# The first block of x is loaded from SyncE's queue, third, and no longer from ScalarE's

## The chip, the cores and the metric

The kernel runs on one core of a Trainium2 chip. The core has five engines that run their own instruction streams: TensorE (PE in the profile; its weight loads are PEld), VectorE (DVE), ScalarE (ACT), GpSimd (POOL) and SyncE (SP). Transfers are issued by an engine into its queue and carried by 16 DMA engines. The metric is the device time of one execution in microseconds (us).

## The reference

A depthwise convolution with a 1x1 window, and then a pointwise one. The depthwise weight is a scale for each channel, so that it can be put into the matrix of the pointwise one.

```python
x: (1, 384, 384, 384) bf16     # 147,456 pixels of 384 channels
dw: (1, 1, 384), pw: (384, 384)
out = xp[:, i:i+H, j:j+W, :] * dw[i, j]          # one tap, k = 1
return jnp.einsum('bhwc,cd->bhwd', out, pw)
```

## The kernel before

The 147,456 pixels are cut into 288 *supertiles* of 512 pixels (384 KB of x, and as much output). A *chunk* is a run of supertiles loaded by one transfer: 1, 1, 2, 2, 4 supertiles, then 26 chunks of 10, then 6, 4, 4, 2, 1, 1. The first chunk is called x0 here, the next x1, and so on. There are three large buffers for x (`Xs`) and three for the output (`Os`), used in turn by groups of 10 supertiles; the last two supertiles have a buffer of their own (`Xl`), loaded by ScalarE.

The weights are prepared on the chip. pw comes by two loads on SyncE: its first 128 rows (L150, 96 KB, semaphore `s_pw`) and the other 256 (L151, 192 KB, `s_pw2`). dw comes by a load on ScalarE (L149). TensorE turns dw into a column (L225), VectorE builds three scaled selection matrices from it (`sel_w`, L310), and TensorE multiplies them with the rows of pw (L245): step k = 0 needs the first load of pw, k = 1 and 2 the second. The products are six pieces in PSUM; ScalarE casts pieces 0, 2, 3, 4, 5 into `w_r` and VectorE piece 1 (L295). Ahead of that TensorE runs matmuls on constants (`idle_work`, L212) that nothing reads.

Each supertile then goes through three engines. VectorE transposes it in two halves (L282, `transposes`), which wait for its chunk's semaphore and for TensorE to be done with the buffer `T` two supertiles before. TensorE does 12 steps of 4 matmuls that work side by side on 32 rows each (L195, `supertile`); the first step waits for the first half of the transpose, for a free PSUM buffer and, in the very first supertile, for pieces 0 to 3 of the weights; pieces 4 and 5 are waited for in later steps. ScalarE copies the PSUM buffer to the output buffer (L332).

SyncE issues all other loads and the stores in one written order: `todo` is sorted by the supertile after which each may go. Loads x1 to x4 go at once; before the first chunk of 10 SyncE waits for x1 to land (L162); then that chunk and the next go, and then 28 waits on a semaphore that is long full (L166), which let SyncE pass without a pause; then stores and loads alternate. A load into a buffer in use waits for the last transpose that reads it (L121), a store for ScalarE's copy (L145). Each engine's transfers go into one queue of its own: SyncE's is q1, ScalarE's q10.

The step that the change touches is the issue of x0 (L152), a call of `load_x` with ScalarE as the issuing engine; without that argument `load_x` issues from SyncE. x0 is waited for by the first transposes.

Of the kernel before, what the change touches and what calls it, by code (L numbers as in the profile page):

```python
# [27 lines left out]
def kernel(  # L28
# [12 lines left out]
    nc = tc.nc  # L41
# [61 lines left out]
    with tc.tile_critical(sync_engine=mybir.EngineType.Pool, no_gpsimd_drain=True):  # L103
        def x_of(t):
            g, i, off, first, L = chunks[t]
            n = first + LONG - NS
            if n >= 0:
                return Xl[:, 4 * n : 4 * n + 4, :], s_xl[n], 16
            n = sum(len(ls) > i for ls in groups[g % NR : g + 1 : NR])
            return Xs[g % NR][:, 4 * off : 4 * (off + L), :], s_x[g % NR][i], 16 * n  # L110

        def load_x(t, eng=nc.sync):
            g, i, off, first, L = chunks[t]
            dst, sem, _ = x_of(t)
            rows = xf[512 * first : 512 * (first + L), :]
            if first + LONG < NS:
                src = rows.rearrange("(p s) c -> p (s c)", p=P)
                dst = dst.rearrange("p s c -> p (s c)")
                if i == 0 and g >= NR:
                    je = g_end[g - NR]  # L120
                    eng.wait_ge(s_t[je % 2][1], je // 2 + 1)  # L121
            else:
                src = rows.rearrange("(a k q) c -> q a k c", k=4, q=4)
            eng.dma_start(dst, src).then_inc(sem, 16)
# [24 lines left out]
        nc.scalar.dma_start(dw_row[:], dw.rearrange("a e c -> a (e c)")).then_inc(s_dw, 16)  # L149
        nc.sync.dma_start(pw_n[:, 0], pw[0:P, :]).then_inc(s_pw, 16)  # L150
        nc.sync.dma_start(pw_n[:, 1:3], pw[P:C, :].rearrange("(k p) d -> p k d", p=P)).then_inc(s_pw2, 16)  # L151
        load_x(0, nc.scalar)  # L152

        todo = []
        for t, (g, i, off, first, L) in enumerate(chunks):
# [214 lines left out]
```

## Time and profile before

| what | us |
|---|---|
| median of 3 runs | 576.95 (576.24 to 577.43) |
| the profiled execution | 577.43 |
| its span, first to last instruction | 575.7 |
| first matmul of L195 | 8.44 |
| last output copies begin | 571.57 |
| TensorE busy | 567.2 (99%) |
| VectorE busy | 507.0 (88%) |
| ScalarE busy | 419.1 (73%) |
| DMA engines, packet time of q1 | 97.2% of 16 engines' span |

A line of the profile's groups gives the line, the engine and the operation, what is written from what, the shape, the count; then busy time and the mean duration in ns; then the idle time of the engine ahead of it and what ended it. A line of the timeline gives the start, the duration and the same names, with the idle time in brackets. In a table by stretches the columns are the stretch, its length, the engine's busy time and its instructions, the clock granted to TensorE (1.00 is full), the busy share of the DMA engines and GB/s. A line of transfers gives the issuing engine (ACTq is ScalarE's sequencer, SPq SyncE's), the count, the KB of each, and the median time from the issue to the landing. A line on a queue gives its packets, its MB and the time that its packets took as a share of the 16 engines' time.

### The profile page before, as it was taken

To read this page: it belongs to the slowest core of one execution; us is meant where nothing else is said; L and a number is where in the kernel's file an instruction comes from. 1 tells how busy PE (TensorE), PEld (TensorE's weight loads), DVE (VectorE), ACT (ScalarE), POOL (GpSimd) and SP (SyncE) were. 2 spreads that over 40 slices of the span, in tenths; PEclk is the share of its full clock that TensorE was granted. 3 is DMA by queue.
4 is the path that set the end of the run, shared out by engine and by line. 5 is a ranking of instruction groups with operands and counts; after the bars stand their busy time and mean duration, and the time that the engine had idled before them with its cause. 6 is when DMAs were issued, how large, how long until landed. Compare 5 with 4: busy or idle time off the path is not lost.

```text
span 575.7 us, 29705 instructions
## 1 busy us (share of the span) xinstructions
PE 567.2 (99%) x13867; PEld 386.3 (67%) x13867; DVE 507.0 (88%) x584; ACT 419.1 (73%) x297; POOL 0.5 (0%) x5
## 2 busy tenths in 40 slices
PE   7999999999999999999999999999999999999997
PEld 3666666666666666666666666666666666666664
DVE  5889888988898888988898889888988898888985
ACT  5777777777777777777777777777777777777775
POOL 0000000000000000000000000000000000000000
PEclk8999999999999999999999999999999999999999
DMA  8999999999999999999999999999999999999677
GB/s 338 420 366 420 425 422 430 440 416 407 394 425 402 385 396 423 396 388 404 431 381 397 404 424 400 388 419 406 395 404 430 388 403 401 419 394 379 265 287 249
DMA packets 26468, 226.88 MB, mean 394 GB/s; under 512 B 1241, under 2 KB 7002, under 8 KB 22618
## 3 DMA queue, kind: packets, MB, share of 16 engines
q1 hardware_dynamic: 25280, 225.61, 97.2%
q10 hardware_dynamic: 1178, 1.18, 0.7%
q14 instruction: 9, 0.07, 0.0%
q8 instruction: 1, 0.02, 0.0%
HBM read 113.54 MB, written 113.25 MB: 394 GB/s over the span
## 4 chain that ended last, share of the span: by engine, by line
PE 97%; DMA 1%; ACT 1%; issue 0%; DVE 0%; DVEq 0%; SPq 0%; POOLq 0%
PE ps L195 97%; DMA pw_n<-in_pw_dram 1%; DMA out_dram<-O 0%; ACT w_r L295 0%; ACT O L332 0%; DVE O L330 0%; DVEq L103 0%; SPq L150 0%; PE ps L245 0%; SPq L365 0%; POOLq L103 0%; POOLq L354 0%
## 5 line engine op out<-in xcount | busy, mean ns | idle before, releaser
L195 PE MATMUL ps<-w_r,T 32*128 32x384 bf16 x13824 | 563.1, 321 | 0.9 <-ACT w_r L295 0.9
L282 DVE STREAM_TRANSPOSE T<-X 128x384 uint32<-128x384 uint32 x572 | 500.2, 875 | 59.3 <-PE ps L195 1.6
L332 ACT CAST O<-ps 128x1536 bf16<-128x1536 f32 x287 | 413.0, 1439 | 148.4 <-PE ps L195 148.4
L195 PEld LDWEIGHTS ps<-w_r,T 32*128 32x128 bf16 x13824 | 384.9, 93 | 179.1 <-issue 1.2
L295 ACT CAST w_r<-ps 128x768 bf16<-128x768 f32 x5 | 3.7, 810 | 2.5 <-PE ps L245 2.5
L245 PE MATMUL ps<-pw_n,sel_w 64*128 64x384 bf16 x16 | 2.0, 369 | 2.3 <-DMA pw_n<-in_pw_dram 2.2
L282 DVE STREAM_TRANSPOSE T<-Xl 128x384 uint32<-128x384 uint32 x4 | 3.5, 876 | 0.4
L330 DVE CAST O<-ps 128x384 bf16<-128x384 f32 x2 | 1.0, 553 | 3.0 <-DMA out_dram<-O 3.0
L245 PEld LDWEIGHTS ps<-pw_n,sel_w 64*128 64x128 bf16 x16 | 0.7, 97 | 3.9 <-DMA pw_n<-in_pw_dram 3.7
L212 PE MATMUL ps<-const-bfloat16-1.0 32*128 32x384 bf16 x24 | 2.2, 516 | 1.1 <-PEq L354 1.1
L270 ACT ACT_TABLE_LOAD x1 | 1.3, 1283 | 1.9 <-POOLq L103 1.9
L212 PEld LDWEIGHTS ps<-const-bfloat16-1.0 32*128 32x128 bf16 x24 | 0.7, 118 | 1.4 <-issue 1.4
L300 DVE TENSOR_REDUCE sel<-eye 128x64 f32<-128x128 bf16 x1 | 0.3, 286 | 1.5 <-POOL eye L260 1.5
L295 DVE CAST w_r<-ps 128x768 bf16<-128x768 f32 x1 | 1.0, 959 | 0.5 <-PE ps L245 0.5
L329 ACT CAST O<-ps 128x384 bf16<-128x384 f32 x2 | 0.9, 482 | 0.5 <-PE ps L195 0.5
L307 DVE COPY dw_f<-ps 128x3 f32<-128x3 f32 x1 | 0.2, 163 | 0.9 <-PE ps L225 0.9
L310 DVE TENSOR_SCALAR sel_w<-sel,dw_f 128x256 bf16<-128x256 f32 x3 | 0.9, 351 | 0.0
L225 PEld LDWEIGHTS ps<-const-bfloat16-1.0,dw_row 1*128 1x128 bf16 x3 | 0.3, 115 | 0.4 <-DMA dw_row<-in_dw_dram 0.4
L260 POOL TENSOR_SCALAR_AFFINE_SELECT eye<-const-bfloat16-1.0 128x128 bf16<-128x128 bf16 x1 | 0.3, 293 | 0.6 <-POOLq L103 0.6
L270 ACT COPY warm<-const-float32-0.0 128x1 f32<-128x1 f32 x2 | 0.3, 188 | 0.0
L225 PE MATMUL ps<-const-bfloat16-1.0,dw_row 1*128 1x1 bf16 x3 | 0.3, 176 | 0.0
L354 POOL MEMSET const-bfloat16-1.0<- 128x1 bf16 x1 | 0.1, 101 | 0.0
(3 smaller groups left out, 0.3 us busy)
## 6 DMA issues: line engine op xcount, KB each, us to landing
X<-in_x_dram SPq DMA_DIRECT2D x26, 3840.0 KB, 21.4
out_dram<-O SPq DMA_DIRECT2D x26, 3840.0 KB, 27.4
X<-in_x_dram SPq DMA_DIRECT2D x3, 1536.0 KB, 17.9
out_dram<-O SPq DMA_DIRECT2D x4, 768.0 KB, 9.2
out_dram<-O SPq DMA_DIRECT2D x2, 1536.0 KB, 14.9
X<-in_x_dram SPq DMA_DIRECT2D x3, 768.0 KB, 8.3
X<-in_x_dram SPq DMA_DIRECT2D x1, 2304.0 KB, 19.6
out_dram<-O SPq DMA_DIRECT2D x1, 2304.0 KB, 11.4
```

Of the source, the lines that this page charges most:

```text
L195: mm = nc.tensor.matmul(PS[s][:, q, :D], lhsT=Ts[s][32 * q : 32 * q + 32, b, par::2], rhs=w_r[32 * q : 32 * q + 32, b, par, :], start=(b, ...
L212: nc.tensor.matmul(PS[0][:, 2 * (i % 2) + i // 2, :D], lhsT=ones[32 * i : 32 * i + 32, 0:P], rhs=ones[32 * i : 32 * i + 32, :], start=True ...
L225: mm = nc.tensor.matmul(PS[1][:, 0, D + k : D + k + 1], lhsT=dw_row[:, P * k : P * k + P], rhs=ones[0:1, 0:1], start=True, stop=True,)
L245: mm = nc.tensor.matmul(PS[(k + 1) % 2][:, 2 * r + v, :D], lhsT=sel_w[64 * v : 64 * v + 64, k, r, :, :].rearrange("p q w -> p (q w)"), rhs ...
L260: nc.gpsimd.affine_select(out=eye[:], in_=ones[:, 0:P], pattern=[[-1, P]], compare_op=mybir.AluOpType.is_equal, fill=0.0, base=0, channel_ ...
L270: nc.scalar.copy(warm[:, s : s + 1], nc.const_aps.tensor(0.0, [P, 1], F32)).then_inc(s_a[s])
L282: ins = nc.vector.transpose(out=Tw[:, 3 * h : 3 * h + 3], in_=Xw[:, :, j, 96 * h : 96 * h + 96].rearrange("p k (b w) -> p b k w", w=32),)
L295: o = nc.vector.tensor_copy(out, in_) if e == 0 else nc.scalar.copy(out, in_)
L310: nc.vector.tensor_scalar_mul(sel_w[:, k], sel[:].unsqueeze(2).to_broadcast([P, 2, 4, 32]), dw_f[:, k : k + 1]).then_inc(s_sw)
L329: nc.scalar.copy(Ov[:, q, j, :], PS[s][:, q, :D]).then_inc(s_a[s])
L330: nc.vector.tensor_copy(Ov[:, q + 1, j, :], PS[s][:, q + 1, :D]).then_inc(s_d)
L332: a = nc.scalar.copy(Ov[:, :, j, :], PS[s][:, :, :D])
```

## The change

x0 is issued by SyncE, after the two loads of pw and before x1, and no longer by ScalarE after dw. SyncE's queue then holds, in this order, pw's first 128 rows, the other 256, x0, x1, x2, x3, x4. ScalarE's first 28 us hold one transfer, that of dw. Nothing else differs: sizes, buffers, semaphores, the matmuls on constants, the 28 waits on SyncE and the order of the waits at the end are the same.

```diff
         nc.scalar.dma_start(dw_row[:], dw.rearrange("a e c -> a (e c)")).then_inc(s_dw, 16)
         nc.sync.dma_start(pw_n[:, 0], pw[0:P, :]).then_inc(s_pw, 16)
         nc.sync.dma_start(pw_n[:, 1:3], pw[P:C, :].rearrange("(k p) d -> p k d", p=P)).then_inc(s_pw2, 16)
-        load_x(0, nc.scalar)
+        load_x(0)
```

## The prediction

> **What bounds the kernel now.** I read the page first (busy shares and the 40 slices), then the chain that ended last in order of time, then the first 15 us by transfers, by engine and by clock. The page says that TensorE is the bound from end to end:
>
> ```profile
> span 575.7 us, 29705 instructions
> PE 567.2 (99%) x13867; PEld 386.3 (67%) x13867; DVE 507.0 (88%) x584; ACT 419.1 (73%) x297; POOL 0.5 (0%) x5
> PE   7999999999999999999999999999999999999997
> PEclk8999999999999999999999999999999999999999
> L195 PE MATMUL ps<-w_r,T 32*128 32x384 bf16 x13824 | 563.1, 321 | 0.9 <-ACT w_r L295 0.9
> ```
>
> The L195 group has 0.9 us of idle time in the whole run, and all of it lies ahead of its first matmul. So every load after the first few is hidden, and a change to the first loads can act only through the moment at which L195 starts and through the clock just after. Only the first slice has a lower clock (the 8 in PEclk). The chain tells what that start waits for:
>
> ```profile
> 1.40 4.98 DMA pw_n<-in_pw_dram
> 6.42 0.35 PE ps L245 x2
> 6.80 1.51 ACT w_r L295 x2
> 8.44 559.21 PE ps L195 x13063
> ```
>
> The second load of pw is issued at 1.40 and lands at 6.37; two steps of the weight preparation (L245) and two casts (L295) follow, and L195 starts at 8.44. The x0 path ends just before it: in the engine timeline its four transposes begin at 6.57.
>
> ```profile
> 1.52 0.37 ACTq L124 DMA_DIRECT2D X<-in_x_dram  x1
> 1.87 6.31 SPq L124 DMA_DIRECT2D X<-in_x_dram  x6
> 6.41 0.76 PEld L245 LDWEIGHTS ps<-pw_n,sel_w 64*128 64x128 bf16 x12 [2.92 <-DMA pw_n<-in_pw_dram]
> 6.57 2.93 DVE L282 STREAM_TRANSPOSE T<-X 128x384 uint32<-128x384 uint32 x4 [1.38 <-DMA X<-in_x_dram]
> ```
>
> The transfers of the first 2.6 us, and the packets of each queue between 2.6 and 4.0 us (q1 is SyncE's queue, q10 ScalarE's):
>
> ```profile
> X<-in_x_dram SPq DMA_DIRECT2D x1, 768.0 KB, 6.9
> X<-in_x_dram ACTq DMA_DIRECT2D x1, 384.0 KB, 5.0
> X<-in_x_dram SPq DMA_DIRECT2D x1, 384.0 KB, 5.5
> pw_n<-in_pw_dram SPq DMA_DIRECT2D x1, 192.0 KB, 5.0
> pw_n<-in_pw_dram SPq DMA_DIRECT2D x1, 96.0 KB, 2.1
> ...
> q10 hardware_dynamic: 72, 0.22, 89.1%
> q1 hardware_dynamic: 176, 0.13, 38.1%
> ```
>
> The last column of the issues is the time to landing: pw's second load 6.4, x0 6.5, x1 1.87 + 5.5 = 7.4, x2 2.37 + 6.9 = 9.2. While pw's second part (256 packets of 768 B) should be moving, x0's 3 KB packets take 89% of the engines' packet time against 38% for q1. The 192 KB of pw thus land no sooner than the 384 KB of x0. The last view is the clock beside matmul time, in stretches of 3.41 us:
>
> ```profile
> 0.90:4.31 3.41, 3.00 (x31) 1.00 0.70 150
> 4.31:7.73 3.42, 1.15 (x12) 1.00 0.94 370
> 7.73:11.14 3.41, 2.70 (x36) 0.50 1.05 441
> 11.14:14.55 3.41, 3.41 (x92) 1.00 1.15 489
> ```
>
> After a stretch with 1.15 us of matmuls the clock is at half for 3.41 us. L195 works in 2.70 us of it (8.44 to 11.14) and so loses 1.35 us. These are TensorE's two start-up costs: waiting to 8.44, and 1.35 us of half clock.
>
> **The change part by part.** The sum is made against the profiled execution, 577.43 us (span 575.7 and 1.7 around it); the median of the three runs, 576.95, is 0.5 lower.
>
> *ScalarE loses one issue.* The 0.37 us at 1.52 go; the table load now starting at 1.93 moves up as much. The next thing ScalarE does for others is the cast at 3.91, which waits for TensorE: worth 0, hidden by that wait.
>
> *SyncE gets one issue, third.* It takes 0.46 us, as x1's did in the same place (1.87). x0 is issued 0.35 us later than now, and the issues of x1 to x4 each move back by 0.46 to 0.50. x1's packets queue behind pw and x0 anyway; the bytes ahead of the end of x1 are the same 1,056 KB in both orders. Its cover is the backlog. SyncE's fillers and the wait for x1 before the first 3,840 KB load stand behind the landing of x1, and the queue has x2 to x4 to move until 16 us: 0.
>
> *pw's second load is no longer interleaved with x0.* No row shows it alone, so I bound it. Early end: pw's first load of 96 KB (128 packets) landed 2.05 us after its issue, at 3.01; the next 192 KB at the 170 GB/s that the table by stretches has for 2.0 to 3.0 us take 1.16 us: landing 4.2. Late end: take from 6.37 only the 384 KB of x0 at the 410 GB/s of the stretch 5.75 to 6.25, 0.96 us: 5.4. I take 4.8, the middle, as neither row is nearer. From landing to L195 it is 2.07 us today (6.37 to 8.44): 6.9, with ends 6.3 and 7.5. ScalarE's casts set a floor: the first starts at 3.91 and they follow every 0.70, so the third ends at 3.91 + 1.40 + 0.80 = 6.1, and 0.14 later (as from 8.30 to 8.44) L195 starts at 6.25.
>
> *x0 goes behind pw on SyncE's queue.* It now has the issue time, place, size and shape that x1 has in the trace, which landed at 7.36 with x0's 384 KB moving beside it. Without those at 410 GB/s: 6.4, the late end. The early end is 0.96 us after pw's early landing: 5.15. The middle is 5.8. The absolute late bound is 7.36 itself. L195 needs 0.03 to start the transpose, 0.87 for it and 0.14 to pass on: 1.04 after landing, 6.8, with ends 6.2 and 7.45 (8.4 for the absolute bound).
>
> A rule of the Trainium skill speaks against the gain: "DMA: Bandwidth & Descriptors", section "Rules for kernel authors", says that spreading transfers over issuing engines doesn't help, since all run on the same 16 engines, and only saves issue time. By it the move saves nothing and costs the issue, so x0 is 0.35 us later and the sum would be 577.43 + 0; the packet shares of q1 and q10 above are what I set against it.
>
> The two paths end within 0.1 us of each other and the later counts: 6.9. The start is 8.44 - 6.9 = 1.54 us sooner (ends 2.14, from 6.3, and 0.94, from 7.5; 0.0 for the absolute bound).
>
> *What is late next.* Supertile 1: x1 landed by 7.36 + 0.9 for its transpose = 8.3, needed at 6.9 + 1.95 = 8.85 (1.95 us is the spacing of the L332 copies in the steady part). Supertile 2: 9.23 + 0.9 = 10.1, needed at 10.8. Supertile 10, first of the 3,840 KB loads: landed 24.96, ready 25.9, needed at 6.9 + 19.5 = 26.4. Each cover is 0.5 us or more, about the 0.48 by which SyncE's issues move back; a start much before 6.5 would be given back here.
>
> *The clock.* The weight preparation (1.15 us) moves to about 4.8 to 5.9, and L195 from 6.9 on adds 0.83 us before 7.73: the stretch 4.31 to 7.73 then holds about 1.98 us of matmuls in 3.41, 58%. The trace has 88% (full clock after it) and 34% (half clock). No row lies between. If the clock holds, the 1.35 us go; if not, L195 works through all 3.41 us at half and loses 1.71, 0.36 more. I take that it holds: the longest gap falls from 2.23 us to about 1.0.
>
> On this the Trainium skill, "TensorE: Matmul & The Clock Gate", section "Why this matters for your kernels", asks for no idle gaps over about 3 us. The trace contradicts it here, 2.23 us and 0.87 us of gap in one stretch having been enough; by the rule the changed kernel keeps its clock, and the sum is the one below.
>
> Sum: 577.43 - 1.54 - 1.35 = 574.54, and I put 574.6.
>
> **The rivals.**
> *B, the clock drops all the same.* For it: 58% is no nearer 88% than 34%. It gives 577.43 - 1.54 + 0.36 = 576.25, just within 0.2% of the median.
> *C, x0 takes x1's time.* Interleaving was not what slowed pw; the low 167 GB/s in the stretch 4.25 to 4.75, with q10 nearly through, speaks for it, since the engines there are short of packets rather than of bandwidth. x0 lands between 6.4 and 7.36, L195 starts at 7.4 to 8.4, the clock loss stays: 576.4 to 577.4, the middle 576.9. The move then does almost nothing.
> *D, slower.* x0 stands behind 256 short packets in one queue and lands late. Each us after 7.40 costs a us (8.44 - 1.04); from 8.55 on it is over 0.2%. The row for it is x2, one issue later on the same queue, which took 6.9 us: 1.87 + 6.9 = 8.8, start 9.8, 578.8. Against it: x2 is twice as large and had 1,056 KB ahead, x0 has 288.
>
> **How the numbers follow.** The likeliest forecast has 0.46, with its own range 573.9 (start 6.3) to 575.1 (start 7.5); B 0.20, C 0.22, D 0.12. The range from 573.6 to 577.1 leaves out the upper end of C, nearly all of D and some 3 in 100 below. About 0.2% (1.15 us) is what a measurement can tell here: faster means below 575.8. That takes nearly all of the first case, 0.44, and the lower edges of B and C, 0.11: 0.55. Same: 0.33, most of B and C. Slower: 0.12.
>
> **What would show it.** Of the changed kernel: no x load on q10 before 27 us; pw's second load landing before 5.4 and x0 after it, before 6.5; the wait ahead of the second group of L245 matmuls below 1.3 us instead of 2.23; L195 starting near 6.9; first PSUM copy (L332) near 8.9 instead of 11.92 if the clock holds, and near 10 if it drops at 7.73 (0.83 us of the supertile's 1.95 done by then, the other 1.12 at half clock). From L195's start on the spacing of 1.95 us and the last 4 us unchanged. I'd be wrong if pw still lands after 6, if x0 lands after 7.4, if the clock is at half from L195's start, or if a later load (x1, x2, the first long one) makes L195 wait.

## The result, and the profile after

The changed kernel takes 574.43 us (median of 6 runs, 573.97 to 574.73) against 576.84 us before in the same session (6 runs, 576.24 to 577.43). The ratio is 0.9958 with a 95% interval of 0.9945 to 0.9970: 2.4 us, or 0.4%, faster. The forecast was 574.6. The profiled execution took 574.73 us, with a span of 573.0.

From the page of the changed kernel, the lines that answer to those shown of before, and the group of the weight preparation (L245), whose mean is of use below:

```profile
span 573.0 us, 29705 instructions
PE 566.9 (99%) x13867; PEld 420.6 (73%) x13867; DVE 507.5 (89%) x584; ACT 418.7 (73%) x297; POOL 0.5 (0%) x5
PEclk9999999999999999999999999999999999999999
L195 PE MATMUL ps<-w_r,T 32*128 32x384 bf16 x13824 | 561.8, 321 | 0.7 <-DVE T L282 0.7
L245 PE MATMUL ps<-pw_n,sel_w 64*128 64x384 bf16 x16 | 2.9, 514 | 0.1
```

TensorE is still the bound, and L195 waits once. What it waits for has changed: the last releaser is the transpose of x0 and no longer the weight cast. The chain says the same:

```profile
1.87 4.20 DMA X<-in_x_dram
...
6.09 0.87 DVE T L282
6.96 0.09 issue
7.05 557.91 PE ps L195 x13728
```

The transfers issued in the first 2.6 us (KB each, then us from the issue to the landing; the two of 384 KB are x0 and x1, and 4.4 is their mean), and what moved between 2.6 and 4.0 us, by queue:

```profile
X<-in_x_dram SPq DMA_DIRECT2D x2, 384.0 KB, 4.4
pw_n<-in_pw_dram SPq DMA_DIRECT2D x1, 192.0 KB, 2.5
pw_n<-in_pw_dram SPq DMA_DIRECT2D x1, 96.0 KB, 2.0
...
q1 hardware_dynamic: 284, 0.28, 91.0%
```

pw's second load takes 2.5 us instead of 5.0 and lands at 3.87 instead of 6.37. In the same 1.4 us SyncE's queue now moves 284 packets; it moved 176 while ScalarE's queue was busy beside it. x0, issued 0.35 us later than before, lands at 6.07 (1.87 + 4.20), 0.5 us sooner.

The 2.70 us between the two profiled executions (577.43 and 574.73) have two parts. L195 starts at 7.05 instead of 8.44: 1.39. From its first matmul to the last output copies it takes 561.83 us (7.05 to 568.88) instead of 563.13 (8.44 to 571.57): 1.30, the clock. From there to the end both take 4.1. The first PSUM copy begins at 9.23, 2.18 us after L195's start; before it was at 11.92, 3.48 us after. The first line is of before, the second of the changed kernel:

```profile
11.92 1.44 ACT L332 CAST O<-ps 128x1536 bf16<-128x1536 f32 x1 [2.22 <-PE ps L195]
9.23 1.44 ACT L332 CAST O<-ps 128x1536 bf16<-128x1536 f32 x1 [1.71 <-PE ps L195]
```

Both profiled executions are the slowest of their six; the medians are 2.41 us apart.

### The profile page after: what moved, and what is told of

The parts are those of the page before. It is cut to its first block, busy times and chain, and to the rows that moved or that the text cites. A ratio compares the mean times of both kernels' runs of the same rounds, so it can differ in the third digit from the quotient of the medians.

```text
span 573.0 us, 29705 instructions
## 1 busy us (share of the span) xinstructions
PE 566.9 (99%) x13867; PEld 420.6 (73%) x13867; DVE 507.5 (89%) x584; ACT 418.7 (73%) x297; POOL 0.5 (0%) x5
## 4 chain that ended last, share of the span: by engine, by line
PE 97%; DMA 1%; ACT 0%; DVE 0%; SPq 0%; issue 0%; DVEq 0%; POOLq 0%
PE ps L195 97%; DMA X<-in_x_dram 1%; DMA out_dram<-O 0%; ACT O L332 0%; DVE T L282 0%; DVE O L330 0%; DVEq L103 0%; SPq L151 0%; SPq L150 0%; SPq L365 0%; POOLq L103 0%; POOLq L354 0%
## 5 line engine op out<-in xcount | busy, mean ns | idle before, releaser
L195 PE MATMUL ps<-w_r,T 32*128 32x384 bf16 x13824 | 561.8, 321 | 0.7 <-DVE T L282 0.7
L195 PEld LDWEIGHTS ps<-w_r,T 32*128 32x128 bf16 x13824 | 419.0, 93 | 143.8 <-issue 1.4
L245 PE MATMUL ps<-pw_n,sel_w 64*128 64x384 bf16 x16 | 2.9, 514 | 0.1
L245 PEld LDWEIGHTS ps<-pw_n,sel_w 64*128 64x128 bf16 x16 | 0.8, 114 | 2.2 <-DMA pw_n<-in_pw_dram 1.2
```

The source lines that it names most:

```text
L195: mm = nc.tensor.matmul(PS[s][:, q, :D], lhsT=Ts[s][32 * q : 32 * q + 32, b, par::2], rhs=w_r[32 * q : 32 * q + 32, b, par, :], start=(b, ...
L245: mm = nc.tensor.matmul(PS[(k + 1) % 2][:, 2 * r + v, :D], lhsT=sel_w[64 * v : 64 * v + 64, k, r, :, :].rearrange("p q w -> p (q w)"), rhs ...
```

## The experiments

Ten runs were made, in three sets; each set has its own runs of the kernel before (medians 577.04, 576.92 and 577.01), and the ratios are taken within a set. Three theories stood for the landing of pw's second load: sharing the DMA engines with a large load (S), which queue that load is on (Q), and later the first packets from x (F); two for the clock: the gap in TensorE's work (G), and chance (P). In the first set S says that x0 disturbs pw from either queue; for the strangers further down it was narrowed to sharing between two queues.

### x0 ahead of pw's second load, all on SyncE

```diff
         nc.sync.dma_start(pw_n[:, 0], pw[0:P, :]).then_inc(s_pw, 16)
+        load_x(0)
         nc.sync.dma_start(pw_n[:, 1:3], ...).then_inc(s_pw2, 16)
-        load_x(0)
```

> Three theories of why pw's second load landed at 6.4 us before and at 3.9 after. S (sharing): x0's packets move on the same 16 engines while pw's are under way, whichever queue they come from. Q (queue): a load on ScalarE's queue disturbs, one on SyncE's doesn't. Here all three stay on SyncE's queue, but x0 goes ahead of pw's second load. S: x0 lands near 5.6 and pw's second load only near 6.0, L195 starts at 6.0 + 2.07 = 8.1, time 575.5 to 576.8. Q: pw's second load lands before 5, L195 starts at 7.1 or sooner, time 574.4 or less.

```profile
X<-in_x_dram SPq DMA_DIRECT2D x2, 384.0 KB, 4.3
pw_n<-in_pw_dram SPq DMA_DIRECT2D x1, 192.0 KB, 3.5
```

```profile
5.42 2.10 PE L245 MATMUL ps<-pw_n,sel_w 64*128 64x384 bf16 x12 [1.23 <-DMA pw_n<-in_pw_dram]
7.61 4.64 PE L195 MATMUL ps<-w_r,T 32*128 32x384 bf16 x84
10.84 1.44 ACT L332 CAST O<-ps 128x1536 bf16<-128x1536 f32 x1 [1.96 <-PE ps L195]
```

576.32 us, ratio 0.9983 (0.9972 to 0.9994). In the engine timeline pw's second step starts at 5.42, L195 at 7.61. x0 lands at 4.50 and its first transpose starts at 5.10, behind VectorE's own weight cast; pw's second load, issued at 1.86, lands at 5.38. Q falls: on SyncE's queue pw is late all the same, when x0 is ahead of it. S has the direction and is 0.6 us too late in size, because in one queue the two loads go one after the other, and both are in by 5.4 us. So the order in the queue decides who is first. The run shows more: behind all 384 KB of x0 in one queue pw's second load landed 1 us sooner than beside them in the kernel before (6.37, and 6.30 in the execution with the fill below), so the bytes alone don't explain the delay there. That two queues also delay the later of the two loads is likely, no more: it landed at 5.2 to 6.3 in the six profiles with both on SyncE's queue, and at 6.3 and 6.5 in the two with x0 on ScalarE's. Of the 1.6 us by which this execution (576.34) is slower than the profiled one of the changed kernel, 0.56 is the later start; the other 1.05 is half clock, for the first copy comes 3.23 us after L195's start.

### pw and x0 all on ScalarE's queue

```diff
-        nc.sync.dma_start(pw_n[:, 0], ...)
-        nc.sync.dma_start(pw_n[:, 1:3], ...)
-        load_x(0)
+        nc.scalar.dma_start(pw_n[:, 0], ...)
+        nc.scalar.dma_start(pw_n[:, 1:3], ...)
+        load_x(0, nc.scalar)
+        nc.sync.wait_ge(s_pw, 16)
```

> pw's two loads and x0 all go on ScalarE's queue behind dw, in this order, and SyncE holds x1 back until pw's first load has landed. S: nothing large moves beside pw, so pw's second load lands 0.5 us later than in the changed kernel (one more issue ahead of it), near 4.4, x0 near 6.6, L195 starts near 7.6, time near 575. Q: pw's second load lands after 5.5 as before, L195 starts after 8, time 576 or more.

575.80 us, ratio 0.9981 (0.9971 to 0.9991); L195 starts at 7.49, x0 lands at 6.5, both as S has it. The time is 0.8 us over S's: the first copy comes 2.79 us after L195's start, so 0.61 of it is half clock, which S's sum had left out. pw's second load landed at 5.25, between the two forecasts (4.4, and over 5.5). Its packets say why: between 2.5 and 4.0 us 376 of pw's 384 packets of 768 B had started, as fast as in the changed kernel, and the other 8 came up to a microsecond later.

```profile
DMA packets 421, 0.33 MB, mean 223 GB/s; under 512 B 30, under 2 KB 406, under 8 KB 421
...
DMA packets 97, 0.27 MB, mean 273 GB/s; under 512 B 2, under 2 KB 10, under 8 KB 97
```

The first line is of 2.5 to 4.0 us, the second of 4.0 to 5.0 (the packets under 512 B have 4 bytes each and carry none of pw's data; the rest under 2 KB are pw's). A load lands with its last packet, and a few stragglers set it. The run doesn't separate S and Q for pw; for x0 and for L195 it goes with S.

### The kernel before, with the gap filled

```diff
             if k == 1:
+                idle_work(7)
                 nc.tensor.wait_ge(s_pw2, 16)
```

> The kernel before, with 28 more matmuls on constants in TensorE's 2.23 us gap, ahead of the wait for pw's second load. Nothing reads them. It measures the clock's part alone. G (gap): the half clock after L195's start comes from the gap; with the gap filled L195 still starts near 8.4, but the clock there is full, and the time falls by about 1.3 us to 575.5. P (chance of phase): the stretches in which the clock is set lie at random against the kernel's start, and the gap plays no part; the time stays at 576.8 and the half clock shows in some executions all the same.

575.86 us, ratio 0.9980 (0.9971 to 0.9989), 1.18 us less than before. L195 starts at 8.37, as before; the first copy comes 2.18 us after it, as at full clock. The runs of before in this set spread from 576.08 to 578.48, those with the fill from 575.68 to 576.35. From the table by stretches (TensorE's busy time follows the length of the stretch):

```profile
2.55:5.96 3.41, 3.34 (x43) 1.00 0.87 268
5.96:9.37 3.41, 2.51 (x47) 1.00 1.03 432
```

G holds: the gap costs about 1.2 us. P may be right in one thing: the chance of the phase may be what made before's times spread, since the spread goes with the gap, from 2.4 us to 0.7; that is argued and not shown.

### The changed kernel with the old gap put back

```diff
             if k == 1:
                 nc.tensor.wait_ge(s_pw2, 16)
+                nc.tensor.wait_ge(x_of(0)[1], 16)
```

> The changed kernel, but the second step of the weight preparation also waits for x0 to land, so that TensorE has the old gap (4.2 to 6.1) while the loads land as in the changed kernel. L195 then starts 2.07 us after 6.07, at 8.1, 1.1 us later than in the changed kernel. G: the clock falls to half after the gap and L195 loses about 1.3 us again, time 574.4 + 1.1 + 1.3 = 576.8. P: only the start counts, 575.5.

576.28 us (575.91 to 578.00), ratio 0.9996 (0.9985 to 1.0006). In the profiled execution x0 landed at 5.19, not 6.07, so that the gap was only 1.1 us and L195 started at 7.47, not 8.1. The clock went to full at 9.32 only. The loads are those of the changed kernel, and most of its gain is gone: the ratio to before is no longer clear of 1. The median lies between the two forecasts (G 576.8, P 575.5), because both took a start at 8.1. The profiled execution, 576.07, decides. Against the 574.73 of the changed kernel its start is 0.42 later, so P gives 575.15 and G, with 1.3 more, 576.45. Its first copy came 3.07 us after L195's start, 0.89 later than at full clock: the clock took twice what the later start did.

```profile
2.50:5.91 3.41, 2.24 (x25) 1.00 0.98 285
5.91:9.32 3.41, 3.33 (x34) 1.00 1.01 403
```

(Before the first recorded change the clock column reads 1.00 by default. The matmuls tell the true one: about 514 ns each for L245 at half clock, about 322 at full.)

### A stranger on ScalarE's queue, from x and from pw

Both keep the changed kernel and add a load that nothing reads.

```diff
         load_x(0)
+        nc.scalar.dma_start(Xl[:96, 0:4, :]..., xf[1024:1408, :]...).then_inc(s_sp, 16)     # from x
+        nc.scalar.dma_start(Xl[:96, 0:4, :]..., pw...).then_inc(s_sp, 16)                   # or from pw
...
             if jj in LONG_AT:
+                nc.scalar.wait_ge(s_sp, 16)
```

> The changed kernel, and beside it ScalarE issues, where x0 was issued before (1.5 us), another load of 288 KB from x in packets of 3 KB, into the buffer Xl, which is free then; nothing reads it. S (sharing between two queues): pw's second load is stretched again, landing after 5.2 instead of 3.9, x0 after 6.3, L195 starts at 7.4 to 8.4, time 575.3 to 576.8. The rival N says that it was x0's own place behind pw that mattered and a stranger on the other queue is harmless: pw's second load near 3.9, L195 near 7.1, time 574.4.

> The same extra load of 288 KB in packets of 3 KB on ScalarE's queue, but read from pw and not from x. S holds for any source: pw's second load after 5.2, L195 at 7.4 to 8.4, time 575.3 to 576.8, as with x as the source. F (first packets from x): it is the slow first packets read from x, up to 1.5 us in this trace's records of both kernels, that hold up pw's packets behind them on the same engine; read from pw the extra load costs little: pw's second load before 4.6, L195 before 7.3, time 574.7 or less.

From x: 576.94 us, ratio 1.0000 (0.9991 to 1.0009). From pw: 577.13 us, ratio 0.9998 (0.9988 to 1.0008). The first two lines are the transfers with the load from x, the others those with the load from pw:

```profile
Xl<-in_x_dram ACTq DMA_DIRECT2D x1, 288.0 KB, 5.1
pw_n<-in_pw_dram SPq DMA_DIRECT2D x1, 192.0 KB, 5.5
```

```profile
Xl<-in_pw_dram ACTq DMA_DIRECT2D x1, 288.0 KB, 4.3
pw_n<-in_pw_dram SPq DMA_DIRECT2D x1, 192.0 KB, 4.6
```

The chain of the execution with the load from x (its lines stand two further down, so that L245 is L247 there and L195 is L197):

```profile
1.40 5.46 DMA pw_n<-in_pw_dram
6.85 0.05 issue
6.90 2.10 PE ps L247 x12
9.00 0.08 issue
9.09 558.69 PE ps L197 x13726
```

pw's second load lands at 6.85 and at 6.02 instead of 3.87, and L195 starts at 9.09 and 8.25. Either stranger takes the whole gain away. F falls: what is read doesn't matter much, only that large packets run in a second queue beside pw's small ones. That it is their size that counts isn't shown, for no stranger with short packets was run. The rival that a stranger is harmless (N in the expectation) falls too. With the stranger from x the start is later than S allowed (8.4): the chain shows that it is pw's landing at 6.85, with 2.10 us of weight preparation at half clock behind it, that sets it; x0, landed at 7.66 and ready 0.87 later, came first.

### pw's first rows on ScalarE's queue

```diff
-        nc.sync.dma_start(pw_n[:, 0], pw[0:P, :]).then_inc(s_pw, 16)
+        nc.scalar.dma_start(pw_n[:, 0], pw[0:P, :]).then_inc(s_pw, 16)
```

> The changed kernel with pw's first 128 rows issued by ScalarE behind dw, so that SyncE issues pw's other rows at 0.96 and x0 at 1.40 instead of 1.87. If x0's landing sets the start of L195, as the chain says: x0 lands 0.47 sooner, near 5.6, L195 starts near 6.6, time 574.0. If two queues at once are what hurts (S): pw's first load on the second queue lands late, after 3.6, the first matmuls on pw and all casts after them are late, and L195 starts at 7.1 or later, time 574.4 to 575.

```profile
X<-in_x_dram SPq DMA_DIRECT2D x2, 384.0 KB, 5.0
X<-in_x_dram SPq DMA_DIRECT2D x1, 768.0 KB, 7.0
pw_n<-in_pw_dram SPq DMA_DIRECT2D x1, 192.0 KB, 2.5
pw_n<-in_pw_dram ACTq DMA_DIRECT2D x1, 96.0 KB, 3.8
```

576.96 us, ratio 1.0003 (0.9994 to 1.0012): slower than the changed kernel in the same set by 2.7, all of the gain. The 96 KB on the second queue take 3.8 us and land at 5.33 (they take 2.0 on SyncE's queue, and 2.0 on ScalarE's too where pw and x0 are all on it, so the queue as such isn't slow); the first matmuls on pw start at 5.37 instead of 3.37, and L195 at 8.26. x0's earlier issue was of no use: it lands at 5.93. S had the direction, and the cost came out several times its forecast of 0 to 0.6: against the first profile of the changed kernel the start is 1.21 us later, and the first copy, 3.20 us after it, shows 1.02 us of half clock, which the forecast left out.

### The changed kernel twice more, and with a fill

```diff
             if k == 1:
+                idle_work(2)
                 nc.tensor.wait_ge(s_pw2, 16)
```

> The changed kernel once more, on the same chip as the others of this set: 574.4, L195 between 6.3 and 7.1 as x0 lands between 5.2 and 6.1.

> The changed kernel on the same chip as the one with the fill: 574.4; if pw's second load lands near 3.9 in this execution, L195 starts by 7.1; if near 5.2, near 7.4.

> The changed kernel with 8 more matmuls on constants ahead of the wait for pw's second load, 0.64 us at half clock. If the changed kernel still loses to the clock in executions whose pw lands late (5.2 instead of 3.9), the fill shortens that gap and lets the clock rise one stretch sooner: median 574.2 and no execution above 575. If the changed kernel has no gap to fill in most executions, the fill only moves the weight preparation back by 0.64 us, which the landing of x0 hides in part: 574.4 to 575.

The changed kernel: 574.30 us in the second set (5 runs), 574.73 in the third (12 runs, 573.94 to 576.68), ratios 0.9954 and 0.9963. With the fill: 574.82 (574.76 to 575.15), ratio 0.9960 (0.9946 to 0.9975). It evens out the time and doesn't lower it: of the 12 unfilled runs four are above 575, of the filled ones one, and the fast ones below 574.7 are gone, as the second half of the expectation had it. No kernel tried here beats the changed one.

The two profiles show in what ways the changed kernel's executions differ. In the second set (576.18 us, the slowest of the five) pw's second load took 3.8 us:

```profile
pw_n<-in_pw_dram SPq DMA_DIRECT2D x1, 192.0 KB, 3.8
```

```profile
2.83:6.24 3.41, 2.29 (x20) 1.00 0.97 312
6.24:9.65 3.41, 3.33 (x38) 1.00 1.05 434
```

It landed at 5.19, again by stragglers: between 3.6 and 4.6 us 9 of pw's packets were still to start, and 6 after that, where the first profile of the changed kernel had none after 3.6. The trace has a reason for the nine: one packet of pw, started at 2.82, took 0.97 us (the median is 0.04), and they start one by one, 0.03 us apart, from its end at 3.80, as if they had stood behind it. For the other six no such packet is on record. TensorE had a gap of 1.05 us, the clock rose at 9.65 only, and L195, started at 7.43, had its first copy at 10.68. In the third set all went well, and the next wait came up:

```profile
6.34 2.13 PE L195 MATMUL ps<-w_r,T 32*128 32x384 bf16 x48 [0.59 <-DVE T L282]
7.96 1.56 DVE L282 STREAM_TRANSPOSE T<-X 128x384 uint32<-128x384 uint32 x2 [1.02 <-DMA X<-in_x_dram]
8.97 3.27 PE L195 MATMUL ps<-w_r,T 32*128 32x384 bf16 x76 [0.50 <-DVE T L282]
```

```profile
0.68:4.09 3.41, 2.90 (x33) 1.00 0.52 145
4.09:7.50 3.41, 2.49 (x46) 1.00 0.99 340
```

The clock is full from 4.09 on. L195 starts at 6.34, is done with the first supertile at 8.47, and then waits 0.50 us for x1, which landed at 7.93. The second copy begins 2.62 us after the first instead of 1.95, so 0.67 of the 0.71 us of the earlier start are given back.

### All profiles side by side

The gap is TensorE's longest wait for pw (for x0 where the old gap was put back); the first copy is counted from L195's first matmul.

| profiled execution | gap | L195 starts | first copy after | time |
|---|---|---|---|---|
| before | 2.23 | 8.44 | 3.48 | 577.43 |
| changed kernel, first | none | 7.05 | 2.18 | 574.73 |
| changed kernel, second set | 1.05 | 7.43 | 3.25 | 576.18 |
| changed kernel, third set | none | 6.34 | 2.18 | 574.70 |
| x0 ahead of pw's second load | 1.23 | 7.61 | 3.23 | 576.34 |
| pw and x0 on ScalarE's queue | 0.96 | 7.49 | 2.79 | 575.78 |
| before, gap filled | none | 8.37 | 2.18 | 576.06 |
| changed, old gap put back | 1.10 | 7.47 | 3.07 | 576.07 |
| stranger from x | 2.71 | 9.09 | 2.95 | 577.53 |
| stranger from pw | 1.87 | 8.25 | 3.91 | 577.64 |
| pw's first rows on ScalarE's queue | 2.08 | 8.26 | 3.20 | 576.96 |
| changed, with a fill | none | 7.28 | 2.18 | 575.15 |

In ten of the twelve the time is that of the first copy plus 565.5 us, to 0.03; the other two (the start at 6.34, and the fill in the changed kernel) lose 0.7 and 0.2 us later on. So the two columns ahead of the time tell where it went. In the eight executions with a gap of 0.96 us or more the first supertile ran in part at half clock; in the four without one it ran at full.

## Why the prediction was right

*What bounds the kernel* was read rightly: both parts of the gain lie before the first copy, and the rest of the run is the same to 0.01 us (the copies stay 1.95 us apart, the tail 4.1).

*pw's second load* was given 4.8, with ends 4.2 and 5.4. It landed at 3.87, before the early end, and in four other profiled executions with the same queue order at 5.19, 3.91, 3.93 (with the gap put back) and 4.39 (with the fill). The cause was right, as the two strangers show. The size was off because the early end took the 170 GB/s of the stretch 2.0 to 3.0 us for the load alone; in 2.6 to 4.0 us the queue moved 0.28 MB, 200 GB/s, and more in the middle of it. The term hardly entered the start: with pw at 3.9 the casts set the floor at 6.25, and x0 counts.

*x0's landing* was given 5.8, with ends 5.15 and 6.4: 6.07 here, 6.16 and 5.36 in the two repetitions. The step from its landing to L195 was given 1.04 and took 0.98. *The start* was given 6.9 and came at 7.05, 0.15 off in the sum. With this and 0.05 on the clock the sum is 577.43 - 1.39 - 1.30 = 574.74, against 574.73 of the profiled execution.

*The clock* was given 1.35 us and brought 1.30, but the picture behind the number was only half right. I wrote that the clock "holds" after 4.31 because the gap gets short. In the profiled execution it was at half all through the weight preparation (L245 took 514 ns, not 369 on average as before) and rose at 6.41, 0.6 us ahead of L195. The stretches lie differently in each execution. What the missing gap does is to make a busy stretch end earlier than L195's first supertile. The experiments that fill the gap and put it back show that the gap is the cause; at which moment the clock rises in an execution without a gap (4.09, 5.83, 5.96, 6.41) is chance.

That this term came out whole is in part luck. By the sum, pw lands at 4.8, and TensorE, done with its first step at 4.19, waits some 0.65 us for it. No profile has such a wait; those of 0.96 to 1.23 us cost 0.6 to 1.1 us of half clock. pw's landing at 3.87, outside the range given for it, left no wait at all. Nor is it shown that a stretch with 58% of matmuls keeps a full clock, as the prediction took it: the lowest share that kept it in these traces is 73% (2.49 of 3.41 us, in the execution that started at 6.34). One reading was off as well: of the 2.23 and 0.87 us of gap "in one stretch", the second ran from 7.57 to 8.44, and the stretch ended at 7.73.

*The rule that I set the packet shares against* (the Trainium skill, "DMA: Bandwidth & Descriptors", "Rules for kernel authors": spreading over issuing engines doesn't help and only saves issue time) is confirmed in its first half and is too mild in the second: the two queues here cost 2.4 us, the clock's part included. The share of a queue in packet time (89% against 38%) was the right line to read.

*Rival B* (L195 at half clock all the same) is what the slowest profiled execution of the changed kernel shows, with late stragglers of pw, though there the clock had not risen yet; it isn't the usual case, for 18 of the changed kernel's 23 runs lie below 575. *Rival C* (the engines were short of packets, so that interleaving was not the cause) falls with the strangers: pw is late again with either, though the engines have more to do. The low 167 GB/s that spoke for it was not at q10's end: 38 of its packets moved between 4.0 and 5.0 us, and 34 more by 6.4. *Rival D* (x0 late in the queue) didn't happen: 6.07 in place of 8.55 or more. *The next wait* was named rightly: a start before 6.5 would be given back at a later load, and the execution that started at 6.34 waited 0.50 us for x1. x1 landed there at 7.93, later than the 7.36 taken as its latest. *The cost of nothing* for ScalarE's lost issue and for SyncE's shifted ones stands: x1 lands at 7.02, x2 at 8.9 and the first long load at 24.5, all somewhat sooner than before.

What stays open: why a packet of 768 B now and then takes up to a microsecond, and why the rest of the stragglers are late. No run shows whether short packets in the second queue would disturb pw as well, or whether x0 held back on ScalarE's queue until pw is in would do as well as on SyncE's.

## What to carry to other kernels

A small load with short packets that starts the chain did best here with the DMA engines to itself for its first microseconds. Try to put the next large load behind it in the same queue and to keep the second queue empty, instead of issuing both at once from two engines. Ahead of the first real matmuls, look at TensorE's gaps as well as at the start: work that nothing reads, put into a gap of 2 us, was worth 1.2 us in one kernel here, and made its time steadier; in the kernel without a gap it gained nothing. Where the first start has been moved up, the next load in the order is the next wait.

## What the runs showed of the hardware

- Two queues at once slowed the short packets by more than the bytes explain: 192 KB landed at 6.37 and 6.30 beside 384 KB of 3 KB packets in the other queue, and at 5.38 behind the same 384 KB in its own. 96 KB of 768-byte packets landed 2.0 us after their issue on the queue that also carried x0 behind them, and 3.8 us when x0 and 192 KB of pw ran on the other queue; 192 KB took 2.5 us with the large loads behind them and 4.6 to 5.5 beside 288 to 384 KB of 3 KB packets.
- The clock is set in stretches of 3.41 us whose place changes from one execution to the next: in the kernel before it changed at 4.31, 7.73 and 11.14, in other executions for the first time at 4.09, 6.41 or 9.65 (the stretches ahead of a first change are counted back from it). A stretch with 2.90 to 3.34 us of matmuls was followed by full clock, one with 2.24 or 2.29 us (66 and 67%) did not raise it from half, one with 2.49 us (73%) kept it at full, and one with 1.15 us lowered it. It was lowered though the longest gap was 2.23 us, so a gap need not be as long as the 3 us of the Trainium skill ("TensorE: Matmul & The Clock Gate", "Why this matters for your kernels").
- The same load in the same order can land 1.3 us later (3.87 and 5.19) because of fifteen packets of 256; nine of them started one by one from the end of a packet that took 0.97 us instead of 0.04.
